# One more turn of ScalarE's tables and a new order of the whole program, in a gated linear attention with a squared-ReLU channel mix on one core

## The chip, the core and the metric

The kernel runs on one core of a Trainium2 chip. Five engines work on their own queues: TensorE (PE in the profile, its weight loads PEld), VectorE (DVE), ScalarE (ACT), GpSimd (POOL) and SyncE (SP), which here only issues transfers between the chip's memory and the core's buffers. The metric is the device time of one execution in microseconds (us). The times shown are medians over runs; the profile is of one execution.

## The reference

Two layers, on 4 sequences of 768 steps with 8 heads of 48 channels, all in float32.

```
f = 1 / (1 + exp(-f_logit))
for t in range(S):
    state = f[t][:, None] * state + outer(k[t], v[t])
    y[t] = q[t] @ state
x = y, heads side by side (384 channels)
xk = mu_k * x + (1 - mu_k) * x_prev;  xr = mu_r * x + (1 - mu_r) * x_prev
out = sigmoid(xr @ w_r) * (maximum(xk @ w_k, 0) ** 2 @ w_v)
```

`x_prev` is `x` one step earlier; w_k is 384 by 1024, w_v 1024 by 384, w_r 384 by 384. The weights come as 64-bit words, of which the kernel makes float32 numbers itself.

## The kernel before

**Attention** is done in 24 chunks of 128 steps, 6 to a sequence. For chunk i a scan on DVE makes the running product b of the gates (`b{i}`, line 223), ACT makes its inverse by a logarithm and an exponential (`ln{i}`, line 229, and `rb{i}`, line 231), DVE corrects that inverse (`n{i}`, line 244, and `iv{i}`, line 246). q is scaled by b on DVE (`q{i}`, line 233), k by the inverse (`k{i}`, two halves, lines 241 and 242, on POOL or DVE). PE then takes the scores (`S{i}`, line 302), transposes of k (`TR{i}`, line 287), state sums (`P{i}`, line 321) and the outputs (`YA{i}`, `YB{i}`, line 334). Around them stand copies and small products: `bl` keeps the last column of b, `kt` brings the transposed k from PE's accumulators, `m` masks the scores (on DVE in one instruction, on ACT as a copy, with the mask then on POOL as `mg`), `zb`, `T`, `g` and `za` carry the state over, `y` writes the output out. `S{i}` waits for both halves of `k{i}` and for `q{i}`; `P{i}` for `kt{i}`.

**Gates.** f is loaded and turned by a sigmoid in place, three chunks at a time. The first three chunks are loaded and turned one by one (`f0.0` to `f0.2`, `sf0.0` to `sf0.2`, line 387), the second three in one piece (`f1`, `sf1`, line 392). The later pieces are turned next to a unit's output sigmoid (`sg{u}`, lines 482 to 487), which loads the sigmoid table before and the table of logarithm and exponential behind it. `ex` (line 772) is the first load of that second table; every `ln` waits for it.

**Channel mix** goes in 8 units of 3 chunks. Per unit PE makes 8 groups F of 9 matmuls (through w_k), 3 groups R of 9 (w_r) and 6 groups W of 12 (w_v), all in line 453: each float32 operand is split in a high part (xh, k2h, H of a weight) and a low one (xl, k2l, L), and three of the four products are taken. For unit 0 the mix of x with its past is done on PE (`XM`, line 583), with the diagonal matrices `dg` (POOL) and `eg`, copied out of `dg` by transfers (`ed`). F's results pass relu (`r`), square (`h`, `kk`) and difference (`l`), which DVE, ACT and POOL share.

**Weights.** Each piece of a weight (8 of wk, 6 of wv, 4 of wr) is loaded and made into numbers by S (ACT or DVE), T and X (DVE), H and L, at 512, 384 or 288 columns for wv, wk and wr. Later a check reads each piece once more (`c{p}` into two buffers "words", `cm{p}` on DVE, line 748); after the last one `lo`, `lot` (two small transposes on PE) and `lom` make a flag (`strong`).

**Order.** ORDER is a table of about 1,400 task names, written out by hand or search; a name with /A, /V or /G puts the task on ACT, DVE or POOL. Each engine issues its instructions in the order of the table, SP its transfers too, and an instruction that waits holds all behind it on its engine. Accumulator tiles `pm` (four of them) and other rotating buffers are handed out in the same order.

Of the kernel before, what the change touches and what calls it, by code (L numbers as in the profile page):

```python
# [52 lines left out]
dg/G b3 q1 ln0 rb0 ln1 bl3/V rb1 n0 iv0 wv2 qk2 n1 q2 iv1 k0/G k1/G wvS2/A qk3 q3 wvT2 wk0 ed2 v2 v1 wk4 S0 ln2 rb2
m0/A n2 wvX2 iv2 TR0 kt0/A wkS0/A S1 P0 zb0/A ln3 m1/A TR1 YA0 w0/A wkT0 wkX0 kt1/A rb3 T0 mg0/G g1 YB0 k2/G za1/G b4
n3 y0/A P1 S2 TR2 zb1 YA1 wk5 wk2 wk1 qk4 v3 ed0 ed1 wk6 wk3 iv3 T1 ln4 wkS5/A bl4/A m2/V wvH3/G mg1/G za2/G wkS2/A
kt2/A wkH0/A P2 rb4 w1/A wkS1/A wkT2 mg2/V wkT5 wkX2 q4 zb2 YB1 n4 T2 wkX5 wkT1 k3/G wkL0/G x00 wvH2/G g3 wkH5/G g4
za3/G iv4 wkX1 wvL3/V wkH1/G TR3 y1/A S3 YA2 kt3/A w2/A wkS4/A P3 YB2 wkS3/A y2/A wkT4 wkT3 wkX4 wkX3 b5 qk5 wr2 wk7
wr0 wr1 wv1 v4 wr3 XM0.00 wkS6/A m3/A ln5 mh0.00/A XM0.10 wkT6 zb3 wkX6 q5 ml0.00 rb5 bl5/A wkH4/A wvS1/A n5 T3 iv5
mh0.10/A wkH3/A ml0.10 wvT1 wvX1 XM0.01 k4/G mg3/G TR4 mh0.01/A wkS7/A YA3 S4 w3/A wvL2/G g5 wkL4/G YB3 kt4/A wrS3/A
P4 wkT7 ml0.01 wkX7 wrS0/A y3/A wvH1/A wkH6/A wkH2/G za4/G k5/G wkL1/G wkH7/G wkL2/G wvL1/G wkL3/G wkL7/G TR5 wrT0  # L60
m4/V wrT3 wrX0 wrX3 kt5/V F0.01 r0.01/A zb4 F0.00 v5 wrS1/A sp0.01 wv5 sp0.00 sp0.02 wv0 f4 v8 YA4 d0.010 wrT1 T4 wrX1
mg4/V xm0.010 za5/V wvS5/V wrH3/A kk0.01/A w4/A P5 S5 YB4 wrH0/A wrH1/G wkL6/G wkL5/G F0.03 d0.011 r0.00/A kk0.00/A
y4/A h0.00 r0.03/A kk0.03/A F0.04 r0.04/A h0.01 d0.012 zb5 xm0.011 wvT5 YA5 wrS2/V wvX5 kk0.04/A w5/A F0.02 xh0.010/V
wrT2 m5/V wrX2 mg5/V YB5 xm0.012 h0.04 xh0.011/A r0.02/A xh0.012/A wvS0/V xl0.010/V wvT0 wvH5/G wrL0/G wvL5/G wrL1/G
l0.00/G x01 wrL3/V xl0.011/V y5/A h0.03 wrH2/A h0.02 wvX0 kk0.02/V xl0.012/G wrL2/V F0.07 F0.06 r0.06/A r0.07/A F0.05
r0.05/A kk0.05/A kk0.07/V R0.0 h0.07 kk0.06/A lg0.0/A h0.05 R0.1 lg0.1/A h0.06 wvH0/G l0.03/G wvL0/G l0.04/G l0.01/G
qk8 qk7 v6 f2 qk6 wv4 l0.02/V wvS4/V wvT4 wvX4 wvH4/A sp1.00 sp1.01 R0.2 d1.00 xm1.010 xh1.010/A lg0.2/A sg0 v7 qk9
sp1.02 c5 f3 W0.20 W0.00 l0.07/G wvL4/G l0.05/G l0.06/V xm1.000 W0.01 d1.01 xm1.001 xm1.011 sf2 d1.02 xm1.002
xh1.000/V xm1.012 xl1.000/G o0.0 b7 W0.10 W0.21 xh1.001/A xl1.001/V q7 b6 bl7/A xh1.011/A xh1.002/A ln6 bl6/A W0.11
xl1.002/G xl1.010/G xh1.012/V o0.2 q6 o0.1 F1.00 F1.02 ln7 rb7 rb6 n6 iv6 k6/V r1.02/V TR6 r1.00/A kk1.00/A h1.00  # L70
kt6/V l1.00/V kk1.02/A xl1.011/G xl1.012/G R1.0 b8 F1.04 r1.04/V lg1.0/A kk1.04/V h1.02 ln8 h1.04 R1.1 R1.2 lg1.1/A n7
bl8/V q8 rb8 n8 iv7 lg1.2/A F1.01 F1.07 P6 S6 iv8 r1.01/V r1.07/V kk1.01/V zb6/V l1.04/V T6 m6/V kk1.07/V mg6/V
l1.02/G k7/G k8/G g8 g7 za7/G F1.03 sg1 TR7 sf3 YA6 w6/V kt7/A r1.03/A b9 S7 YB6 P7 F1.05 TR8 y6/A h1.01 m7/V zb7
mg7/V q9 ln9 YA7 kt8/A w7/A rb9 r1.05/A bl9/A h1.03 kk1.03/V T7 S8 YB7 P8 F1.06 b10 h1.07 kk1.05/A ln10 y7/A v10 qk10
qk11 v9 n9 iv9 za8/V zb8 m8/V T8 b11 mg8/V l1.01/G l1.03/G cz k9/G r1.06/A kk1.06/A h1.06 bl10/V W1.10 TR9 YA8 S9 w8/A
rb10 g10 g9 x02 za9/G kt9/V YB8 P9 q10 q11 h1.05 l1.05/V y8/A ln11 bl11/A rb11 l1.06/G l1.07/V n10 zb9 iv10 W1.20
W1.11 W1.21 W1.00 W1.01 n11 iv11 T9 o1.1 m9/A out0.0 qk12 v11 sp2.00 d2.00 xm2.000 xh2.000/A xm2.010 sp2.01 out0.2
sp2.02 out0.1 d2.01 d2.02 xm2.001 xm2.011 o1.2 k10/G k11/G za10/G TR10 TR11 xh2.010/A xh2.001/A YA9 kt10/A w9/A
xl2.000/V S10 P10 g11 mg9/G YB9 xl2.001/G xm2.002 xh2.002/A xl2.002/V kt11/V zb10 xm2.012 xh2.012/V xl2.010/V F2.00
r2.00/A T10 F2.07 xl2.012/V o1.0 m10/V mg10/V F2.01 F2.04 kk2.00/A y9/A h2.00 r2.04/V YA10 w10/V kk2.04/A h2.04 P11  # L80
S11 YB10 F2.02 y10/A F2.03 za11/V l2.00/V r2.07/V zb11 kk2.07/V YA11 h2.07 r2.01/A kk2.01/A r2.02/A h2.02 l2.04/V
m11/V mg11/V l2.07/G xh2.011/V w11/V F2.05 h2.01 YB11 r2.03/V kk2.02/V l2.01/V x03 xl2.011/G h2.03 kk2.03/A l2.02/G
R2.0 y11/A lg2.0/V R2.1 lg2.1/A r2.05/A h2.05 F2.06 kk2.05/V r2.06/V l2.05/V R2.2 h2.06 lg2.2/A out1.0 v12 f5 out1.1
out1.2 qk13 f6 v13 qk14 v14 qk15 sp3.00 sp3.02 sp3.01 sg2 d3.00 l2.03/G kk2.06/V xm3.010 xm3.000 W2.10 l2.06/G W2.11
W2.20 d3.01 xh3.010/V xl3.010/V d3.02 xm3.011 sf4 xh3.000/A xm3.012 xm3.002 xm3.001 xh3.012/A W2.21 W2.00 b12 W2.01
ln12 bl12/A rb12 xh3.011/A o2.1 xl3.012/G q12 o2.2 n12 xl3.011/G xl3.000/G iv12 k12/V TR12 R3.0 b14 o2.0 kt12/A
xh3.001/A bl14/A b13 ln13 lg3.0/V xh3.002/A q14 bl13/V xl3.001/V q13 R3.2 R3.1 rb13 ln14 lg3.2/A rb14 S12 P12 n13
lg3.1/V m12/V iv13 mg12/V xl3.002/G k13/G g14 g13 n14 F3.03 r3.03/V F3.00 TR13 iv14 F3.04 k14/V zb12/V kk3.03/V kt13/V
T12 TR14 r3.04/V kt14/V sg3 YA12 P13 S13 r3.00/A w12/A YB12 F3.02 F3.01 sf5 h3.00 kk3.00/A za13/G m13/V mg13/V
kk3.04/V zb13 b15 T13 r3.02/V b16 l3.00/G za14/G y12/A h3.03 ln15 bl15/V g15 g16 YA13 kk3.02/A h3.04 w13/A S14 P14  # L90
rb15 h3.02 YB13 v15 qk16 v17 F3.07 q15 m14/V r3.01/V kk3.01/A n15 zb14 T14 mg14/V iv15 x04 l3.03/G l3.02/G y13/A h3.01
F3.05 F3.06 r3.05/A r3.07/V h3.07 ln16 rb16 za15/V kk3.07/V bl16/V r3.06/A h3.06 kk3.06/A h3.05 k15/G TR15 YA14 w14/V
S15 YB14 kt15/V P15 m15/A kk3.05/A y14/A l3.01/G l3.04/V q16 l3.07/G l3.06/V l3.05/V n16 b17 bl17/V iv16 zb15 W3.20
W3.00 W3.21 W3.01 out2.2 out2.0 qk17 sp4.00 sp4.02 sp4.01 v16 mg15/G T15 q17 o3.2 f7 c2 out2.1 k16/G g17 TR16 kt16/A
YA15 w15/A d4.00 xm4.010 xm4.000 o3.0 d4.01 d4.02 xm4.001 xm4.012 xm4.002 ln17 xh4.010/A xh4.000/A xh4.002/A S16 P16
YB15 W3.10 W3.11 xl4.000/G xh4.001/V y15/A rb17 m16/V xl4.001/V n17 iv17 xm4.011 xl4.002/G za16/G F4.00 F4.03 r4.03/A
# [926 lines left out]
```

## Time and profile before

| | us |
|---|---|
| time, median of 3 runs | 340.57 (337.43 to 342.58) |
| the profiled execution, in all | 339.45 |
| its span | 337.7 |
| PE busy | 309.6 (92%) |
| PE weight loads busy | 296.5 (88%) |
| DVE busy | 271.9 (81%) |
| ACT busy | 200.1 (59%) |
| POOL busy | 141.3 (42%) |

The span runs from the first instruction to the end of the last work; the time in all has what lies around it too. A busy share is an average over the span: in its first 16 us PE does nothing, and in the long middle it is busy throughout. The mean granted clock of TensorE is 0.998 of full speed.

### The profile page before, as it was taken

Reading aid. Unit: us, or ns where it says so; the run is one execution under the profiler, and the core shown is the slowest. Engines: PE = TensorE matmul, PEld = TensorE weight load, DVE = VectorE, ACT = ScalarE, POOL = GpSimd, SP = SyncE. Lnnn points to the kernel's source line nnn. Section 1 sums busy time; section 2 is a strip of 40 time slices with the busy share of each in tenths; the row PEclk is TensorE's granted clock in tenths of the full one; section 3 lists DMA queues with packets and bytes.
Section 4 is the critical chain, followed back from the end, with each engine's and each line's share of the span. In section 5 each row is a group of like instructions: output and inputs, shape, how many; then the busy total and the mean of one; then the engine's idle time right before and its main releaser. Section 6 shows DMA issues by size and latency. Waiting matters only on the chain.

```text
span 337.7 us, 10736 instructions
## 1 busy us (share of the span) xinstructions
PE 309.6 (92%) x4458; PEld 296.5 (88%) x4458; DVE 271.9 (81%) x519; ACT 200.1 (59%) x427; POOL 141.3 (42%) x184
## 2 busy tenths in 40 slices
...
GB/s 246 384 264 237 318 127 411 214 107 2 1 90 170 92 53 365 120 1 2 14 203 22 209 2 215 199 82 0 2 211 156 4 64 48 112 68 213 136 99 105
DMA packets 20634, 45.32 MB, mean 134 GB/s; under 512 B 2848, under 2 KB 13024, under 8 KB 20576
## 3 DMA queue, kind: packets, MB, share of 16 engines
...
HBM read 38.54 MB, written 4.72 MB: 128 GB/s over the span
## 4 chain that ended last, share of the span: by engine, by line
PE 82%; DMA 8%; DVE 3%; issue 3%; SPq 1%; POOL 1%; ACT 0%; DVEq 0%; POOLq 0%
PE pm L453 63%; PE py L334 8%; DMA qk<-in_qkt 4%; PE pss L302 4%; PE pm L287 3%; DMA words<-in_wk 3%; PE pm L583 2%; PE pss L321 2%; DMA out<-t 1%; DVE pm L525 1%; DVE t L545 1%; SPq L381 0%; POOL dg L761 0%; DVE dg L748 0%; DVE t L507 0%
## 5 line engine op out<-in xcount | busy, mean ns | idle before, releaser
L453 PE MATMUL pm<-xh,wk 128*128 128x384 f32 x384 | 104.8, 339 | 0.5 <-DVE t L629 0.5
L453 PE MATMUL pm<-wv,k2h 128*128 128x384 f32 x384 | 97.0, 333 | 0.4 <-DVE t L545 0.3
L453 PEld LDWEIGHTS pm<-xh,wk 128*128 128x128 f32 x384 | 69.3, 188 | 2.4 <-DVE t L629 0.8
L453 PEld LDWEIGHTS pm<-wv,k2h 128*128 128x128 f32 x384 | 68.3, 188 | 1.2 <-DVE t L545 0.6
L453 PE MATMUL pm<-wv,k2l 128*128 128x384 f32 x192 | 63.6, 331 | 0.0
L453 PE MATMUL pm<-xl,wk 128*128 128x384 f32 x192 | 63.6, 331 | 0.0
L635 POOL TENSOR_TENSOR k2l<-t,k2h 128x384 fp32r<-128x384 f32 x36 | 39.1, 1097 | 57.3 <-ACT k2h L627 44.7
L560 POOL TENSOR_TENSOR xl<-t,xh 128x384 fp32r<-128x384 f32 x25 | 26.4, 1064 | 59.8 <-ACT xh L553 42.6
L453 PE MATMUL pm<-wr,xh 128*128 128x384 f32 x144 | 36.5, 334 | 0.0
L453 PEld LDWEIGHTS pm<-xl,wk 128*128 128x128 f32 x192 | 36.1, 188 | 0.0
L453 PEld LDWEIGHTS pm<-wv,k2l 128*128 128x128 f32 x192 | 36.0, 188 | 0.0
L627 ACT ACTIVATE k2h<-t 128x384 fp32r<-128x384 f32 x64 | 32.5, 521 | 5.8 <-DVE t L623 5.6
L622 ACT ACTIVATE t<-pm 128x384 f32<-128x384 f32 x37 | 17.7, 489 | 30.6 <-PE pm L453 28.4
L302 PE MATMUL pss<-qk 64*64 64x64 f32 x768 | 17.2, 228 | 17.4 <-POOL qk L241 16.2
L302 PEld LDWEIGHTS pss<-qk 64*64 64x64 f32 x768 | 14.5, 141 | 18.4 <-POOL qk L241 16.2
L223 DVE TENSOR_TENSOR_SCAN pm<-f,low 128x512 f32<-128x512 f32 x24 | 30.2, 1262 | 0.2
L453 PEld LDWEIGHTS pm<-wr,xh 128*128 128x128 f32 x144 | 25.5, 188 | 0.2
L241 POOL TENSOR_TENSOR qk<-qk,rb 128x256 f32<-128x256 f32 x17 | 13.7, 806 | 27.2 <-DVE rb L246 27.1
L366 ACT ACTIVATE x<-py 64x128 f32<-64x128 f32 (+1 forms) x63 | 19.5, 309 | 9.1 <-PE py L334 8.1
L553 ACT CAST xh<-t 128x384 fp32r<-128x384 f32 x32 | 15.9, 511 | 14.9 <-DVE t L545 14.8
L545 DVE SCALAR_TENSOR_TENSOR t<-pm,mu_sb,x 128x384 f32<-128x384 f32 x42 | 24.2, 609 | 0.4
L453 PE MATMUL pm<-wr,xl 128*128 128x384 f32 x72 | 23.9, 332 | 0.0
(127 smaller groups left out, 597.9 us busy)
## 6 DMA issues: line engine op xcount, KB each, us to landing
...
```

What stands on the lines that cost most here:

```text
L223: pl.add(f"b{i}", ("V", lambda: nc.vector.tensor_tensor_scan(b().rearrange(FL), f().rearrange(FL), self.low.rearrange(FL), 1.0, op0=ALU.mu ...
L241: e.tensor_tensor(k()[:, ::2], k()[:, ::2], rb()[:, ::2], op=ALU.mult)
L302: nc.tensor.matmul(self.pss[HALF[h], r, 64 * j : 64 * j + 64], k()[HALF[r], j, HALF[h]], q()[HALF[r], j, HALF[h ^ j % 2]], start=True, sto ...
L334: first[c, h] = nc.tensor.matmul(to, lhs, rhs, start=(c, h) not in first, stop=stop, skip_group_check=True)
L366: e.activation(o, i_, AF.Copy, scale=-1.0)
L453: nc.tensor.matmul(lines(ps), lhs(a, j), lines(rhs(bb, j)), start=ends[0] and i == 0, stop=ends[1] and i == len(pr) - 1)
L545: pl.add(f"xm{u}.{p}{w}{j}", ("V", lambda xm=xm, w=w, j=j: nc.vector.scalar_tensor_tensor(xm(), pm("d", u, p, j), self.mu_sb[:, w, j : j + ...
L553: pl.add(f"xh{u}.{p}{w}{j}", ("A", lambda xm=xm, hi=hi: nc.scalar.copy(hi(), xm())), ("V", lambda xm=xm, hi=hi: nc.vector.tensor_copy(hi() ...
L560: e.tensor_tensor(lo(), xm(), hi().bitcast(F32), op=ALU.subtract)
L622: pl.add(f"r{name}", ("A", lambda: nc.scalar.activation(r(), ps(), AF.Relu)), ("V", lambda: nc.vector.tensor_scalar(r(), ps(), 0.0, None, ...
L627: pl.add(f"h{name}", ("A", lambda: nc.scalar.activation(hi(), r(), AF.Square)), after=[f"r{name}"], **(kw | {"uses": kw["uses"] + [("t", " ...
L635: e.tensor_tensor(lo(), kk(), hi().bitcast(F32), op=ALU.subtract)
```

## The change

Two rules of the plan change. `ex`, the first load of the table of logarithm and exponential, waits for `sf0.2` and no longer for `sf1`. `sf1` waits for `ex` and loads that table again behind itself; as the sigmoid stands in another table, a load of the sigmoid's table comes ahead of it too. The table ORDER is replaced by another with the same 1,406 tasks, in which many tasks have another place, and some another engine.

```diff
 ORDER = """
-f0.0 f0.1 sf0.0 b0 mu wv3 f0.2 sf0.1 sf0.2 f1 b1 sf1 ex wvS3/V wvT3 onemu wvX3 b2 bl0/V qk0 v0 qk1 bl2/A q0 bl1/V g2
+f0.0 sf0.0 f0.1 sf0.1 b1 bl1/A b0 mu f0.2 qk0 sf0.2 qk1 ex ln1 rb1 bl0/V onemu b2 q0 q1 f1 n1 ln0 iv1 rb0 n0 iv0 k0/V
...
             if u < AHEAD:
-                pl.add(f"sf{u}", ("A", lambda: nc.scalar.activation(t(), t(), AF.Sigmoid)), after=[f"f{u}", "sf0.2"])
+                def late():
+                    nc.scalar.activation(t(), t(), AF.Sigmoid)
+                    nc.scalar.preload_act_table_set(EXP_SET)
+
+                pl.add(f"sf{u}", ("A", late), after=[f"f{u}", "ex"])
...
         pl.add("ex", ("A", lambda: nc.scalar.preload_act_table_set(EXP_SET)),
-               after=["sf1"])
+               after=["sf0.2"])
```

ACT's list at the program's start, before (f_61 holds the first three chunks' gates, f_62 the next three; rb the inverses, pm the accumulator tiles in which b stands):

```order
L869 ACT_TABLE_LOAD
L387 ACTIVATE f_61<-f_61 128x512 x3
L392 ACTIVATE f_62<-f_62 128x1536
L772 ACT_TABLE_LOAD
L226 COPY bl<-pm_96 128x4
L229 ACTIVATE rb_97<-pm_93 128x512
L231 ACTIVATE rb_97<-rb_97 128x512
```

and in the changed kernel:

```order
L873 ACT_TABLE_LOAD
L387 ACTIVATE f_61<-f_61 128x512 x2
L226 COPY bl<-pm_93 128x4
L387 ACTIVATE f_61<-f_61 128x512
L776 ACT_TABLE_LOAD
L229 ACTIVATE rb_97<-pm_93 128x512
L231 ACTIVATE rb_97<-rb_97 128x512
L229 ACTIVATE rb_98<-pm_94 128x512
L231 ACTIVATE rb_98<-rb_98 128x512
L393 ACT_TABLE_LOAD
L393 ACTIVATE f_62<-f_62 128x1536
L394 ACT_TABLE_LOAD
```

The large sigmoid on f_62 has moved from ahead of the first logarithm to behind the second exponential, with a load on either side of it; chunk 1 comes ahead of chunk 0.

DVE's list from the first scan on, before (qk holds q and k of a chunk, words a piece of a weight):

```order
L223 SCALAR_TENSOR_TENSOR pm_93<-f_61,low 128x512
L223 SCALAR_TENSOR_TENSOR pm_94<-f_61,low 128x512
L685 TENSOR_SCALAR pm_95<-words_122 128x512
L673 SCALAR_TENSOR_TENSOR pm_95<-words_122,pm_95 128x512
L756 TENSOR_SCALAR one_mu<-mu_sb 128x6
L681 SCALAR_TENSOR_TENSOR words_122<-words_122,pm_95 128x512
L223 SCALAR_TENSOR_TENSOR pm_96<-f_61,low 128x512
L227 COPY bl<-pm_93 128x4
L233 TENSOR_TENSOR qk_64<-qk_64,pm_93 128x512
L227 COPY bl<-pm_94 128x4
L223 SCALAR_TENSOR_TENSOR pm_95<-f_62,low 128x512
L233 TENSOR_TENSOR qk_65<-qk_65,pm_94 128x512
```

and in the changed kernel:

```order
L223 SCALAR_TENSOR_TENSOR pm_95<-f_61,low 128x512
L233 TENSOR_TENSOR qk_64<-qk_64,pm_94 128x512
L233 TENSOR_TENSOR qk_65<-qk_65,pm_93 128x512
L244 TENSOR_TENSOR pm_93<-rb_97,pm_93 128x512
L246 SCALAR_TENSOR_TENSOR rb_97<-pm_93,rb_97 128x512
L244 TENSOR_TENSOR pm_94<-rb_98,pm_94 128x512
L246 SCALAR_TENSOR_TENSOR rb_98<-pm_94,rb_98 128x512
L241 TENSOR_TENSOR qk_64<-qk_64,rb_98 128x2x128
L242 TENSOR_TENSOR qk_64<-qk_64,rb_98 128x2x128
L309 TENSOR_TENSOR ss_99<-pss,mask 128x512
L233 TENSOR_TENSOR qk_66<-qk_66,pm_95 128x512
L223 SCALAR_TENSOR_TENSOR pm_93<-f_62,low 128x512
```

These rows begin at the third scan; the two ahead of it are those of before, with a copy of bl and one_mu behind them. The three instructions on the weight piece words_122 have left, the scan on f_62 has moved behind the first scores' mask, and the scaling of chunk 0's k (lines 241 and 242), which was POOL's, stands here.

SP's list of transfers at the start, before:

```order
L381 DMA f_61<-in_zt 128x512 x2
L755 DMA mu_sb<-in_mu 128x6
L666 DMA words_122<-in_wv 128x1024
L381 DMA f_61<-in_zt 128x512
L381 DMA f_62<-in_zt 128x1536
L211 DMA qk_64<-in_qkt 128x1024
L213 DMA v_103<-in_vt 128x384
L211 DMA qk_65<-in_qkt 128x1024
```

and in the changed kernel:

```order
L381 DMA f_61<-in_zt 128x512 x2
L759 DMA mu_sb<-in_mu 128x6
L381 DMA f_61<-in_zt 128x512
L211 DMA qk_64<-in_qkt 128x1024
L211 DMA qk_65<-in_qkt 128x1024
L381 DMA f_62<-in_zt 128x1536
L213 DMA v_103<-in_vt 128x384
L211 DMA qk_66<-in_qkt 128x1024
```

The weight piece is gone from between the slices of f, and both first qk tiles stand ahead of the second piece of f. An element has four bytes: 128x512 is 256 KB.

## Rows read from the trace of the kernel before

**Rows 1.** Busy time by stretch: from:to, length, then PE, PEld, DVE, ACT, POOL, clock, DMA.

```profile
16.20:46.10 29.90, 24.25 (x631) 20.71 (x632) 25.53 (x49) 22.03 (x58) 24.03 (x35) 1.00 0.79 250
46.10:79.40 33.30, 33.01 (x350) 31.76 (x349) 30.50 (x54) 26.97 (x60) 24.95 (x25) 1.00 0.57 205
79.40:312.50 233.10, 233.10 (x3371) 225.70 (x3369) 190.07 (x364) 136.13 (x289) 80.28 (x103) 1.00 0.31 98
312.50:332.40 19.90, 19.27 (x111) 18.31 (x110) 11.33 (x22) 5.98 (x10) 7.04 (x6) 1.00 0.41 127
...
4.70:46.10 41.40, 24.25 (x631) 20.71 (x632) 36.01 (x66) 28.56 (x68) 27.32 (x39) 1.00 0.85 287
```

**Rows 2.** Timeline, PE's first instructions: start, us, what, [idle before and its releaser].

```profile
16.23 0.49 PE L302 MATMUL pss<-qk 64*64 64x64 f32 x8 [16.23 <-POOL qk L241]
```

**Rows 3.** Timeline of ACT from its first sigmoid.

```profile
3.52 1.28 ACT L387 ACTIVATE f<-f 128x512 f32<-128x512 f32 x2 [1.49 <-DMA f<-in_zt]
7.93 0.63 ACT L387 ACTIVATE f<-f 128x512 f32<-128x512 f32 x1 [3.12 <-DMA f<-in_zt]
9.79 1.48 ACT L392 ACTIVATE f<-f 128x1536 f32<-128x1536 f32 x1 [1.24 <-DMA f<-in_zt]
11.29 1.28 ACT L772 ACT_TABLE_LOAD   x1
12.59 0.16 ACT L226 COPY bl<-pm 128x4 f32<-128x4 f32 x1
12.65 0.60 ACT L229 ACTIVATE rb<-pm 128x512 f32<-128x512 f32 x1
13.28 0.63 ACT L231 ACTIVATE rb<-rb 128x512 f32<-128x512 f32 x1
```

**Rows 4.** Timeline of DVE, POOL and PE around the first scores.

```profile
4.74 2.35 DVE L223 TENSOR_TENSOR_SCAN pm<-f,low 128x512 f32<-128x512 f32 x2
...
11.11 0.69 DVE L233 TENSOR_TENSOR qk<-qk,pm 128x512 f32<-128x512 f32 x1 [0.46 <-DMA qk<-in_qkt]
...
13.94 0.70 DVE L244 TENSOR_TENSOR pm<-rb,pm 128x512 f32<-128x512 f32 x1 [0.29 <-ACT rb L231]
...
14.68 0.69 DVE L246 SCALAR_TENSOR_TENSOR rb<-pm,rb 128x512 f32<-128x512 f32 x1
15.28 0.69 DVE L244 TENSOR_TENSOR pm<-rb,pm 128x512 f32<-128x512 f32 x1
...
15.45 0.73 POOL L241 TENSOR_TENSOR qk<-qk,rb 128x256 f32<-128x256 f32 x1 [0.89 <-DVE rb L246]
...
16.91 0.92 PE L302 MATMUL pss<-qk 64*64 64x64 f32 x24 [0.19 <-POOL qk L242]
...
17.77 1.11 PE L287 MATMUL pm<-ident,qk 128*128 128x128 f32 x4
...
19.72 0.86 PE L321 MATMUL pss<-v,ktk 64*48 64x48 f32 x32
```

**Rows 5.** Groups of instructions of DVE by line: count, busy us, mean ns, idle before.

```profile
L292 DVE COPY ktk<-pm 128x384 f32<-128x384 f32 x9 | 4.9, 548 | 0.1
...
L241 DVE TENSOR_TENSOR qk<-qk,rb 128x256 f32<-128x256 f32 x7 | 3.3, 476 | 0.2
L242 DVE TENSOR_TENSOR qk<-qk,rb 128x256 f32<-128x256 f32 x7 | 3.2, 461 | 0.0
L685 DVE TENSOR_SCALAR pm<-words 128x512 int32<-128x512 int32 x4 | 2.7, 687 | 0.1
...
L673 DVE SCALAR_TENSOR_TENSOR pm<-words_k2h,pm 128x384 int32<-128x384 int32 x4 | 2.2, 556 | 0.0
```

**Rows 6.** The chain that ended last, in the tail: start, us, what.

```profile
301.49 5.40 DMA words<-in_wk
...
312.91 0.69 DVE dg L748
...
313.62 3.92 DMA words<-in_wk
...
319.53 8.42 PE pm L453 x48
```

146 lines of the change are left out of this document (73 added, 73 removed).

## Prediction

> **What bounds the kernel now.** I read the busy times by stretch first, then what PE waited for, then the first 20 us engine by engine, and the tail last. Up to 16.2 us PE does nothing [rows 2]. The stretches behind tell the case [rows 1]. From 16.2 to 46.1 us, where the first attention chunks run and the weights are made, PE is busy 24.25 of 29.90 us, DVE 25.53. From 46.1 us, the first F group of unit 0, PE is busy 33.01 of 33.30, then 233.10 of 233.10, then 19.27 of 19.90; behind 332.4 there are only the last elementwise product and its store. The granted clock is 1.00 in all stretches with PE work. So behind 46.1 us PE is the bound, and PE's work is the same set of matmuls before and after. Its idle time lies in front: 16.2 us in one wait for POOL's scaled k [rows 2], 5.65 us up to the first F, and 0.3 + 0.6 us later. A new order can earn there and hardly elsewhere. In front the busiest engine is DVE: from 4.7 to 46.1 us it is busy 36.01 of 41.40 us [rows 1].
>
> The first wait is a chain. The transfer of the third slice of f lands for 7.93 us, that of f1 for 9.79; ACT takes both sigmoids, loads the table of Ln and Exp from 11.29 to 12.57, and only then begins the first Ln [rows 3]. DVE then makes n and iv, POOL the scaled k, PE starts at 16.23 [rows 4].
>
> **The change part by part.** *The table behind the third sigmoid.* f1's sigmoid (1.48 us, its wait of 1.24 us for the transfer, [rows 3]) leaves the chain. I walk the new chain with the old durations. The first two sigmoids end at 4.80 as now (3.52 + 1.28). Two scans take 2.35 us [rows 4]: b1 from 4.80 ends about 6.0, b0 about 7.15. ACT copies bl1 behind b1, to 6.2. The transfers now stand in the order f0.0, f0.1, f0.2 (256 KB each), qk0, qk1 (512 each), f1 (768). The landings of the old order, where 512 KB of wv3 stood behind the second slice and 768 of f1 ahead of qk0, give the pace: there 512 KB had landed by 4.15, 1280 by 7.93, 2560 by 11.11 [rows 3, 4]. Read at the new sums, f0.2 (768 KB) lands about 5.4, qk0 (1280) 7.9, qk1 (1792) 9.2, f1 (2560) 11.1. So: third sigmoid 6.2 to 6.8, table to 8.1, ln1 and rb1 to 9.35 (0.60 and 0.63 [rows 3]), ln0 and rb0 to 10.55. DVE: b2 from 7.35, q0 8.5, q1 9.2 with its transfer; n1 9.8, iv1 10.5, n0 11.1, iv0 11.9, by the steps of 0.74 from n to iv and 0.60 to the next n [rows 4]. k0 is now DVE's: 0.48 for its first half against POOL's 0.73 [rows 4, 5]. First scores at about 13.1 instead of 16.23: 3.1 us earlier.
>
> *The second unit's sigmoid with its own table turn.* Behind rb0 ACT now has a load, the sigmoid, a load: 1.28 + 1.48 + 1.28 from 10.55 to 14.6, f1 having landed at 11.1. That is 2.57 us more work on ACT. Behind it stand ln2, kt0 and rb2. kt0 needs TR0, which ends about 15.5 (scores 0.92 us from k0's end at 13.5, then the transposes 1.1 [rows 4]), and b3 needs the sigmoid only when DVE gets to it at about 15.7. So the block is hidden by DVE's n, iv and k0 and by PE's scores; without that cover it costs up to its 4.04 us. ACT's total bears it: it is busy 22.03 of 29.90 us in the next stretch [rows 1]. The first state sums, at 19.72 now [rows 4], come at about 16.
>
> Here the Trainium skill speaks against the change. The trace shows a load of 1.28 us, ACT's next instruction 0.02 us behind it and no standstill [rows 3]. ScalarE: Activation LUTs, section "What ACT_TABLE_LOAD costs", adds a drain of about 1380 ns and books 2.66 us for each switch; section "Rules for kernel authors" says to finish one set before switching. By the page's figure the two added switches cost 5.3 us instead of 2.57 and the sum would be some 3 us worse.
>
> *The order up to the first F.* SP held six transfers, four of weights, behind the eg copies, which wait for dg, and dg stood behind POOL's g2, which needs b2; now it stands behind g1, which needs only the first two scans. Ahead of the first F group DVE's list loses wvS3, kt5, m2 and wvL3 to ACT and POOL (0.69 + 0.55 + 0.69 + 0.69) and the merges wkT6, wkX6, wkX4, wrT0, wrX0 to later (3 x 0.55 + 2 x 0.42); it gains k0 (0.48 + 0.46), m0 (0.69) and wrT2 (0.42); two of the small bl copies go and two come [rows 4, 5] (estimates: m and wvL by other instructions of their 128x512, wr by 288 of wk's 384 columns). 5.1 less 2.0 is 3.1 us. One wait is new: m0, now DVE's, waits for the scores from 13.5 to 14.5: 1.0. One is gone: q0's 0.46 us for its transfer [rows 4]. Net 2.5 to 2.6 us. The chain of attention allows 3.1, DVE 2.5; the later decides: first F 2.5 us earlier, at about 43.6. Bounds: nothing (below), and the whole DVE idle of this stretch, 41.40 - 36.01 = 5.4 us, if the new order packs it without a gap.
> S5 (32 matmuls: 24 of them took 0.92 us where k came in halves, an upper bound; taken as 0.5) stands ahead of the first F and no longer behind it: 0.5 us of PE work less from there.
>
> *The rest.* From the first F on PE has no idle to give: 0.3 us to 79.4, none to 312.5. Many evictions go from DVE to ACT (relu 27 to 19 on DVE, squares 33 to 26, differences 28 to 25; 18 of about 0.55 us: some 10): DVE is busy 190.07 and ACT 136.13 of 233.10 us there, so the move uncovers nothing; cost 0, bounds 0 and the price of a new stall, not seen in any row of before. Tail: same work, 0.6 us to win.
>
> Sum: 2.5 + 0.5 = 3.0 us off the span of 337.7, so 334.7. The profiled execution took 339.45 in all, 1.75 more than its span: **336.5 us**. It lies 1.1 us below the median of the runs shown (340.57; they spread from 337.43 to 342.58).
>
> **The rivals.**
> 1. *DVE binds, nothing is won* (338.5 to 340). From the start to unit 1's first F 23 instructions leave DVE's list and 21 come, about 13 us each way (an estimate by the mean durations of their lines): what left ahead of the first F is made up behind it, by four more of the differences l0 and two of wkL among others. DVE's idle from 4.7 to 79.4 is 5.4 + 2.8 = 8.2 us [rows 1] and has to fall to 5.7 for my sum. For it: DVE has 2.8 idle of 33.3 in that stretch. Against: what is added there (l0.05 and on) is needed only by the second half of W0, with six products of 2 us in between.
> 2. *More is won* (332 to 335): DVE's gaps close by 5 us instead of 2.5. For it: attention runs 3 us ahead and weights are loaded earlier, so fewer waits on DVE. Against: PE's and ACT's own chains set some of the gaps.
> 3. *Slower: the check loads in the tail.* Behind the last W6 product DVE's list has cm10, cm0, cm8, r7.00; each c load needs the buffer freed by the check two before it, so cm10, cm8, cm3, cm11, cm13 is a chain of four transfers, and lot on PE waits for its end with three products behind it. Each turn is 3.92 + 0.69 us now [rows 6], four make 18.4, and cm1 and the reductions add about 2 to lot. PE has 8 F, 3 R and 3 W groups in the same time, about 23 us by 8.42 us for 48 matmuls [rows 6], so 2 to 3 us to spare. With the 5.40 us that one such load took beside stores [rows 6], the chain is 5.9 longer: with 2 to spare PE waits 3.9 us, 340.4, above the 339.45 of now. It costs from 4.4 us a load on and turns the sign at about 5.2.
> 4. *ACT stands still as long again behind each of three early loads*: kt0 at about 18.5, first sums at 19, as now; about 339.5. This is the mechanism of the page's drain (ScalarE: Activation LUTs). The 0.02 us between load and next instruction speaks against it.
> That the change does not do what it says is excluded by ACT's rows: one load pair more, and the first Ln behind the third sigmoid.
>
> **How the numbers follow.** My forecast 0.48, rival 1 0.25, rival 2 0.15, rival 3 0.09, rival 4 0.03. The range 332.0 to 340.5 takes in the first four but for the far ends of 2 and 3 (0.08 below and 0.1 above, with the spread of the runs); the likeliest case alone is 335 to 338. A measurement of this kernel can tell about 2% from no change: under 333.8 is faster, over 347.4 slower. Faster takes most of rival 2: 0.13. Slower needs a stall of over 8 us that no row shows, 0.04. The rest, 0.83, is within 2%.
>
> **What would show it.** Right: PE's first matmul at 13 to 13.5 us; the table load at about 7, the second pair around 10.5 to 14.6 with no wait of PE put down to kt; first F matmul between 42.5 and 44.5; from there to the last W no PE idle beyond 1 us. Wrong: first F at 46 with DVE busy throughout (rival 1), a PE wait of over 1 us at lot or at F7 put down to the checks (3), a gap behind ACT_TABLE_LOAD of 1 us or more (4), or stretches behind 46 us in which PE is under 97% busy.

## The result

The changed kernel takes 343.32 us (median of 20 runs, 341.83 to 349.5), the kernel before beside it 340.01 us (20 runs, 337.43 to 343.25). The ratio is 1.012 with a 95% interval of 1.009 to 1.015: slower by 1.2%, where 336.5 us and a range up to 340.5 had been forecast. The ratios, here and in the table below, leave out the few runs that took over 1.5% more than the fastest of their kernel, so they are not the quotients of the medians. The profiled span is 341.9 us against 337.7.

The stretches of the changed kernel, by the same cuts as [rows 1] (columns as there):

```profile
0.00:16.20 16.20, 2.20 (x36) 1.75 (x36) 12.68 (x30) 11.01 (x13) 5.79 (x18) 1.00 0.84 303
16.20:46.10 29.90, 26.47 (x633) 23.00 (x633) 26.75 (x51) 22.27 (x56) 20.71 (x30) 1.00 0.73 237
46.10:79.40 33.30, 31.81 (x310) 29.90 (x309) 30.60 (x60) 28.77 (x61) 19.87 (x23) 1.00 0.55 186
79.40:312.50 233.10, 229.97 (x3345) 220.91 (x3344) 181.97 (x348) 136.47 (x288) 93.13 (x111) 1.00 0.32 102
```

PE now works 2.2 us of the first 16.2, where it did nothing. But behind 46.1 us it has lost 1.2 us up to 79.4 (31.81 against 33.01) and 3.1 us in the long middle (229.97 against 233.10), where it had never stood still. The granted clock is 1.00 in all four rows.

The start of the new kernel, ACT's timeline (compare [rows 3]):

```profile
3.49 1.28 ACT L387 ACTIVATE f<-f 128x512 f32<-128x512 f32 x2 [1.46 <-DMA f<-in_zt]
6.07 0.16 ACT L226 COPY bl<-pm 128x4 f32<-128x4 f32 x1 [1.30 <-DVE pm L223]
6.52 0.63 ACT L387 ACTIVATE f<-f 128x512 f32<-128x512 f32 x1 [0.29 <-DMA f<-in_zt]
7.17 1.28 ACT L776 ACT_TABLE_LOAD   x1
8.46 0.60 ACT L229 ACTIVATE rb<-pm 128x512 f32<-128x512 f32 x1
...
10.89 1.28 ACT L393 ACT_TABLE_LOAD   x1
12.18 1.48 ACT L393 ACTIVATE f<-f 128x1536 f32<-128x1536 f32 x1
13.68 1.28 ACT L394 ACT_TABLE_LOAD   x1
```

and PE's first instructions (compare [rows 2, 4]):

```profile
14.00 1.25 PE L302 MATMUL pss<-qk 64*64 64x64 f32 x32 [14.00 <-DVE qk L241]
15.19 1.11 PE L287 MATMUL pm<-ident,qk 128*128 128x128 f32 x4
16.23 1.13 PE L302 MATMUL pss<-qk 64*64 64x64 f32 x32
18.14 0.90 PE L321 MATMUL pss<-v,ktk 64*48 64x48 f32 x32 [0.77 <-DMA v<-in_vt]
```

The first logarithm runs at 8.46 us instead of 12.65, the first scores at 14.00 instead of 16.23, the first state sums at 18.14 instead of 19.72. So the front does what the change says.

Then the waits. PE's from 46.1 us on (engine, line, what it waited for: us in total, times, longest):

```profile
PE pm L457 <- DVE t L544: 1.3, 1, 1.3
PE pm L457 <- DVE t L511: 1.2, 2, 0.9
PE py L334 <- DVE done L353: 1.0, 1, 1.0
PE py L334 <- issue: 0.7, 1, 0.7
```

In order of time they end at 54.7 (1.3 us), 101.1 (0.7, put down to nothing that the profile shows), 192.0 (1.0), 200.9 (0.3) and 232.4 us (0.9). And DVE's over the whole span, the two kinds that are new:

```profile
DVE pm L529 <- DMA x<-stage: 8.0, 5, 3.0
...
DVE t L511 <- DMA out<-t: 2.9, 1, 2.9
```

But for the one at 101.1, PE waits for DVE, and DVE for transfers: for the spread copies `sp` (six for a unit, 24 KB each, which bring y from the tile "stage" into x, where `d`, line 529, reads them), and for an output store, whose tile t the next output product (line 511) needs. The stop at 54.7 comes of a weight's transfer (e13).

To see where each run loses, I read from each trace when PE begins the first scores and the first F, and when it ends the last W product of units 0, 2, 4 and 7 (us). The experiments e1 to e15 are told below; the median of the kernel before, run beside them, lies between 338.9 and 340.4, and the last column has the ratio to it. The other columns are read from one execution of each kernel. Its time lies within 1 us of the median in most; but in e1, e7 and e15 it is 2.5, 2.1 and 1.6 us below, in e6 1.9 us above, so spans and medians do not rank these alike.

| run | scores | F | W0 end | W2 end | W4 end | W7 end | span | median, ratio |
|---|---|---|---|---|---|---|---|---|
| before | 16.2 | 46.1 | 79.6 | 153.7 | 227.7 | 332.4 | 337.7 | 340.01 |
| after | 14.0 | 45.4 | 80.2 | 155.2 | 231.5 | 336.3 | 341.9 | 343.32, 1.012 |
| e1 table alone | 16.3 | 47.9 | 82.0 | 156.2 | 230.2 | 335.1 | 339.8 | 344.19, 1.013 |
| e2 order alone | 16.8 | 47.3 | 84.0 | 157.9 | 234.4 | 339.3 | 344.5 | 345.65, 1.015 |
| e3 spreads first | 13.0 | 43.8 | 80.6 | 154.8 | 241.2 | 345.5 | 351.3 | 353.12, 1.039 |
| e4 before, spreads late | 16.5 | 44.9 | 79.0 | 153.1 | 233.1 | 337.9 | 343.0 | 345.49, 1.018 |
| e5 two spreads | 13.9 | 44.3 | 79.2 | 153.2 | 231.1 | 336.5 | 342.1 | 344.34, 1.010 |
| e6 new, then old | 12.9 | 43.9 | 82.1 | 157.9 | 231.9 | 336.4 | 342.8 | 342.74, 1.007 |
| e7 old, then new | 17.0 | 45.2 | 79.2 | 153.1 | 229.4 | 334.5 | 340.2 | 344.10, 1.008 |
| e8 v0 and wr1 | 13.2 | 44.1 | 82.1 | 156.3 | 232.5 | 337.5 | 343.0 | 345.61, 1.015 |
| e9 spreads and stores | 14.2 | 45.1 | 79.6 | 153.5 | 228.6 | 332.4 | 338.0 | 339.91, 1.000 |
| e10 stores | 12.9 | 43.9 | 78.5 | 153.7 | 228.1 | 332.8 | 338.3 | 340.70, 1.005 |
| e11 before, no merges | 16.3 | 43.7 | 76.6 | 151.4 | 225.5 | 330.2 | 336.7 | 338.28, 0.997 |
| e12 after, no merges | 14.5 | 45.6 | 79.1 | 155.2 | 231.8 | 337.6 | 343.0 | 344.21, 1.013 |
| e13 f2 late | 13.0 | 44.3 | 77.1 | 151.4 | 228.7 | 333.7 | 339.3 | 341.89, 1.007 |
| e14 all mended | 14.0 | 44.9 | 77.7 | 152.0 | 227.5 | 331.3 | 337.8 | 338.63, 0.995 |
| e15 f2 late, no merges | 13.3 | 43.8 | 76.6 | 150.7 | 227.0 | 332.1 | 337.4 | 340.80, 1.002 |

The change's 4.2 us of span are, by stretch: 0.6 up to the end of W0, 0.9 from there to W2, 2.3 to W4 (76.3 against 74.0), 0.1 to W7, 0.3 behind it. Up to W0 a trace moves by 1 to 2 us with nothing changed there: before and e4 have the same order so far (79.6 and 79.0), and so have after, e3, e5, e9 and e10 (78.5 to 80.6). So the 0.6 us up to W0 is within the scatter. From W2 to W4 the traces repeat: 76.2 to 76.6 us in after, e2, e7, e8, e12 and e15 and 77.3 in e13, all with the new list there; 74.0 to 74.1 in before, e1, e6 and e11, with the old one.

### The profile page after: what moved, and what is told of

The parts are those of the page before. It is cut to its first block, busy times and chain, and to the rows that moved or that the text cites. A ratio compares the mean times of both kernels' runs of the same rounds, so it can differ in the third digit from the quotient of the medians.

```text
span 341.9 us, 10745 instructions
## 1 busy us (share of the span) xinstructions
PE 314.3 (92%) x4458; PEld 298.8 (87%) x4458; DVE 266.1 (78%) x512; ACT 207.5 (61%) x433; POOL 147.4 (43%) x186
## 4 chain that ended last, share of the span: by engine, by line
PE 75%; DMA 8%; DVE 7%; SPq 4%; ACT 3%; issue 2%; DVEq 0%; ACTq 0%
PE pm L457 56%; PE py L334 7%; PE pm L287 3%; PE pss L302 3%; DMA v<-in_vt 3%; DMA x<-stage 3%; PE pm L587 2%; PE pss L321 2%; DMA out<-t 2%; SPq L438 1%; SPq L211 1%; DVE t L511 1%; DVE x L368 1%; DVE t L549 1%; SPq L381 1%
## 5 line engine op out<-in xcount | busy, mean ns | idle before, releaser
L457 PE MATMUL pm<-xh,wk 128*128 128x384 f32 x384 | 104.8, 339 | 1.6 <-DVE t L544 1.3
L639 POOL TENSOR_TENSOR k2l<-t,k2h 128x384 fp32r<-128x384 f32 x39 | 41.6, 1075 | 59.5 <-ACT k2h L631 37.7
L564 POOL TENSOR_TENSOR xl<-t,xh 128x384 fp32r<-128x384 f32 x27 | 31.5, 1185 | 57.2 <-ACT xh L557 24.9
L626 ACT ACTIVATE t<-pm 128x384 f32<-128x384 f32 x45 | 21.8, 489 | 26.7 <-PE pm L457 16.8
L457 PE MATMUL pm<-wr,xh 128*128 128x384 f32 x144 | 36.8, 336 | 0.9 <-DVE t L511 0.9
L223 DVE TENSOR_TENSOR_SCAN pm<-f,low 128x512 f32<-128x512 f32 x24 | 32.2, 1346 | 0.3
L557 ACT CAST xh<-t 128x384 fp32r<-128x384 f32 x31 | 15.1, 512 | 24.7 <-DVE t L549 24.6
L334 PE MATMUL py<-qk,z 64*64 64x64 f32 x704 | 22.7, 235 | 1.4 <-DVE done L353 1.0
## 6 DMA issues: line engine op xcount, KB each, us to landing
v<-in_vt SPq DMA_DIRECT2D x24, 192.0 KB, 4.7
out<-t SPq DMA_DIRECT2D x21, 192.0 KB, 4.4
```

The costliest lines, as they stand in the source:

```text
L223: pl.add(f"b{i}", ("V", lambda: nc.vector.tensor_tensor_scan(b().rearrange(FL), f().rearrange(FL), self.low.rearrange(FL), 1.0, op0=ALU.mu ...
L334: first[c, h] = nc.tensor.matmul(to, lhs, rhs, start=(c, h) not in first, stop=stop, skip_group_check=True)
L457: nc.tensor.matmul(lines(ps), lhs(a, j), lines(rhs(bb, j)), start=ends[0] and i == 0, stop=ends[1] and i == len(pr) - 1)
L557: pl.add(f"xh{u}.{p}{w}{j}", ("A", lambda xm=xm, hi=hi: nc.scalar.copy(hi(), xm())), ("V", lambda xm=xm, hi=hi: nc.vector.tensor_copy(hi() ...
L564: e.tensor_tensor(lo(), xm(), hi().bitcast(F32), op=ALU.subtract)
L626: pl.add(f"r{name}", ("A", lambda: nc.scalar.activation(r(), ps(), AF.Relu)), ("V", lambda: nc.vector.tensor_scalar(r(), ps(), 0.0, None, ...
```

## The experiments

**e1 and e2: the two parts alone.** e1 keeps the old order and makes the new table turn; of ORDER only the names that must move do so:

```diff
-... f0.2 sf0.1 sf0.2 f1 b1 sf1 ex ... b2 bl0/V qk0 v0 ... b3 q1 ln0 rb0 ln1 bl3/V rb1 n0 ... k0/G k1/G ...
+... f0.2 sf0.1 sf0.2 ex qk0 f1 b1 ... b2 bl0/V v0 ... q1 ln0 rb0 ln1 rb1 sf1 n0 ... k0/G k1/G b3 bl3/V ...
```

> The two rules of the plan as in the change, on the old order, with only these tasks moved: ex and qk0 up behind the third sigmoid, sf1 behind rb1, b3 and bl3 behind k1. Theory (the loss sits in the new order's list of transfers, behind unit 1): first scores 1 to 2 us earlier than 16.2, part of it lost by the first F; time 339 to 341 beside 340 of before. Rival (the table turn itself costs: 2.57 us more on ACT, later b3): 342.5 or more.

344.19 us: the theory missed, and the rival's figure came. The first scores did not come earlier, and the state sums came 3.0 us later (22.75 against 19.72). ACT in e1:

```profile
14.76 0.63 ACT L231 ACTIVATE rb<-rb 128x512 f32<-128x512 f32 x1
15.41 1.28 ACT L393 ACT_TABLE_LOAD   x1
16.70 1.49 ACT L393 ACTIVATE f<-f 128x1536 f32<-128x1536 f32 x1
18.21 1.28 ACT L394 ACT_TABLE_LOAD   x1
...
21.67 0.48 ACT L291 COPY ktk<-pm 128x384 f32<-128x384 f32 x1
```

and PE:

```profile
17.82 1.11 PE L287 MATMUL pm<-ident,qk 128*128 128x128 f32 x4
21.87 1.13 PE L302 MATMUL pss<-qk 64*64 64x64 f32 x32 [2.94 <-issue]
```

The block of load, sigmoid and load stands bare: it ends at 19.49, kt0 (the copy at 21.67) comes behind it, and the sums wait. This is the cover of the prediction's second step, taken away. And on DVE chunk 1's q waits for its transfer, with chunk 0's n (14.02) behind it, so the earlier logarithms reach the scores no sooner:

```profile
13.41 0.69 DVE L233 TENSOR_TENSOR qk<-qk,pm 128x512 f32<-128x512 f32 x1 [1.58 <-DMA qk<-in_qkt]
```

By the spans of the traces e1 costs 2.1 us, by the medians 4.2. e2 is the new order with the old turn (f1 behind f0.2, sf1 ahead of ex):

```diff
-... f0.2 qk0 sf0.2 qk1 ex ln1 ... q1 f1 n1 ... ed0 sf1 TR0 ...
+... f0.2 f1 qk0 sf0.2 qk1 sf1 ex ln1 ... q1 n1 ... ed0 TR0 ...
```

> The new order with the old rules for the tables (f1 and sf1 ahead of ex, one table load less), nothing else changed. Theory: first scores at 16 to 17 us, but the same PE waits at 190 and 229 us; 342.5 to 345. Rival (the table turn costs): back to 340.

345.65 us, just above the range expected, with 76.5 us from W2 to W4 (76.3 in the changed kernel). So by the traces' spans the table turn is worth 2.6 us within the new order (scores at 14.0 against 16.8), though the intervals of the two ratios overlap (1.009 to 1.015 and 1.007 to 1.023); in the old order, placed as in e1, it costs 2 to 4 us. The loss behind W2 belongs to the order.

**e3, e4 and e5: where the spread copies stand in SP's list.** In the changed kernel sp4.01 and sp4.02 stand behind v16 and f7 (192 and 768 KB), sp5.02 behind v20, c5 and qk19. e3 moves those and the copies of units 2 and 3 forward, e5 (run later) only those of units 4 and 5; e4 moves the same three backward in the kernel before.

```diff
 e3, e5
-sp4.00 v16 f7 sp4.01 sp4.02 c7 ... sp5.00 sp5.01 v20 c5 qk19 ... sp5.02
+sp4.00 sp4.01 sp4.02 v16 f7 c7 ... sp5.00 sp5.01 sp5.02 v20 c5 qk19
 e3 besides
-sp2.00 out0.2 ... sp2.01 ... v11 sp2.02 ... qk12 qk14 v15 qk15 qk13 v13 ... v12 sp3.00 sp3.02 f4 out1.2 out1.1 ... sp3.01
+sp2.00 sp2.01 sp2.02 out0.2 ... sp3.00 sp3.02 sp3.01 qk12 qk14 v15 qk15 qk13 v13 ... v12 f4 out1.2 out1.1
 e4
-sp4.00 sp4.02 sp4.01 v16 ... f7 ... sp5.00 sp5.01 v18 sp5.02 c4 qk18 qk19
+sp4.00 v16 ... f7 sp4.02 sp4.01 ... sp5.00 sp5.01 v18 c4 qk18 qk19 sp5.02
```

> The changed kernel with the small x<-stage copies of units 2 to 5 moved ahead of the bulk transfers that stand between them in SP's list; no engine's compute order changes. Theory: DVE's 8.0 us of waits for x<-stage fall to 2 or less, the two PE waits of 1.1 us each at 190 and 229 us go; 340.5 to 341.5 beside 343.3 of the change. Rival (these waits are hidden, the loss is DVE's or ACT's order): 343.

> The kernel before with the second and third x<-stage copy of unit 4 moved behind f7 and the third of unit 5 behind qk19 in SP's list, as the new order has them. Theory: DVE waits 3 us or more for x<-stage, where it waited none, and PE waits 1 to 2.5 us near 185 and 225 us; 341 to 342.5. Rival: 340, DVE's wait is covered.

> The changed kernel with three transfers moved in SP's list and nothing else: unit 4's spread copies sp4.01 and sp4.02 stand right behind sp4.00 again (ahead of v16 and f7), sp5.02 right behind sp5.01 (ahead of v20, f and qk19). Theory (the new order's loss behind unit 1 comes in good part from 24 KB spread copies that now queue behind transfers of 768 KB, so that DVE stands still and PE after it): the 1.15 us of PE at S16 to YB15 and the 1.09 us at W4.01 to R5.0 go, and x<-stage waits of DVE fall from 8.0 to under 4 us; 341.0 to 342.0 us, 1.3 to 2.3 us under the changed kernel. Rival (the late copies only show where DVE would wait anyway; the moves of units 2 and 3 were not what made the earlier test slow): no change or slower, 343 us or more.

e4: 345.49 us, the direction expected and 3 us above the range. One copy is enough: DVE's longest wait there and PE's behind it (200 to 235 us):

```profile
DVE pm L525 <- DMA x<-stage: 4.7, 1, 4.7
```

```profile
PE pm L453 <- DVE t L545: 3.9, 1, 3.9
```

From the end of that stop on the granted clock of TensorE is at half, 1.2 GHz:

```profile
223.00:226.40 3.40, 3.20 (x10) 3.20 (x11) 3.40 (x7) 0.93 (x2) 2.08 (x2) 0.50 0.02 5
```

PE begins its matmuls 0.32 us apart there and 0.17 behind it, which adds about 1.6 us to the 3.9. So the price of the late copy is part stop and part clock.

e3: 353.12 us, a miss by 12. DVE's waits for spread copies fell from 8.0 to 2.5 us, but SP's own waits show the price (SP's queue, first in the changed kernel, then in e3, and DVE's in e3 from 130 to 215 us):

```profile
SPq L438 <- DVE stage L368: 30.5, 3, 21.6
```

```profile
SPq L438 <- DVE stage L368: 58.3, 4, 25.4
```

```profile
DVE t L549 <- DMA out<-t: 7.7, 1, 7.7
...
DVE t L511 <- DMA out<-t: 4.0, 1, 4.0
```

A copy put forward waits for its y, and SP holds all that stands behind: the stores came late, their t tiles were not free, and DVE stood still for those. PE stopped for 4.5 us ahead of 159.4 and for 2.8 us ahead of 209.3, and here too the granted clock is at half around the end of each stop, for 6.8 us from 158.1 and 3.4 us from 209.3:

```profile
159.30:164.90 5.60, 5.55 (x17) 5.55 (x18) 5.53 (x9) 1.94 (x5) 4.94 (x7) 0.50 0.10 35
```

By the same steps of 0.32 and 0.17 us the clock makes about 4 of the 10 us that e3 loses from W2 to W4 against the changed kernel, the stops the rest.

e5: 344.34 us, above the range expected. The 1.15 us of PE at unit 5's attention went as expected (W2 to W3 took 41.2 us instead of 42.3), the second (at W4.01 to R5.0) did not, and PE's stop at 200.9 grew from 0.3 to 3.2 us. DVE in e5:

```profile
193.89 0.69 DVE L233 TENSOR_TENSOR qk<-qk,pm 128x512 f32<-128x512 f32 x1
200.00 0.56 DVE L511 TENSOR_TENSOR t<-pm,lg 128x384 f32<-128x384 f32 x1 [5.42 <-DMA out<-t]
```

and SP's issues from 190 to 200 us there (size, median us to landing):

```profile
words<-in_wk SPq DMA_DIRECT2D x1, 512.0 KB, 9.2
v<-in_vt SPq DMA_DIRECT2D x1, 192.0 KB, 8.4
out<-t SPq DMA_DIRECT2D x1, 192.0 KB, 9.1
```

The product at 200.00 is o3.0. The order in which tiles are handed out gives it the tile that out3.2 frees, and that store was issued behind qk17, f6, v19, v17 and c2 (2.1 MB) and landed 9.1 us later. A second wait of 2.5 us is o4.1's, for the tile of out2.0, stored 70 us after it was made.

**e6 and e7: halves of the two orders.** e6 has the new order up to the first R group of unit 0 and all else in the old order, e7 the mirror with the old table turn:

```diff
 e6
-(new order) ... R0.0 R0.2 wvT4 ...
+(new order up to here) R0.0 (what is left, in the old order) ...
 e7
-(old order) ... R0.0 h0.07 kk0.06/A ...
+(old order up to here) R0.0 (what is left, in the new order) ...
```

> The changed kernel's order up to the first R product of unit 0 (at about 60 us), and from there the remaining work in the order of the kernel before; the new table turns are kept. Theory (gain of under 1 us in front, loss of about 4 us behind, so the two are separate): 338.5 to 340.5 us, 3 to 5 us under the changed kernel, and PE waits behind 80 us as small as in the kernel before (some 4 us in all). Rival (the loss behind comes of how the front leaves the queues, and follows it): 342 us or more.

> The mirror of the run before: the order and the table turns of the kernel before up to the first R product of unit 0, from there the remaining work in the new order. Theory (the loss lies in the new order behind unit 1): 343 to 345 us, with PE waits at S16 to YB15, at F4.05 to F4.00 and at W4.01 to R5.0 as in the changed kernel. Rival (the loss comes with the front): 340 to 341 us.

e7, 344.10 us, has the 76.3 us from W2 to W4, e6 the old 74.0: the loss of 2.3 us there belongs to the later list and to nothing ahead of it. e6 as a whole, 342.74 us, lies above the 338.5 to 340.5 expected, where its rival had it, but not for the rival's reason: the stretch from W2 to W4 does not follow the front. W0 ends at 82.1, with PE stops of 1.5 us at 53.5 and at 60.5 and 0.9 at 75.7. The one at 60.5 is in e2, e3 and e8 too, which have no seam; what the seam itself costs is not separated.

**e8: two early transfers.**

```diff
-... f1 n1 ... v1 qk2 wk2 q2 qk3 v0 ... f2 sp0.01 ml0.01 wr1 ...
+... f1 v0 n1 ... v1 qk2 wk2 q2 qk3 ... wr1 f2 sp0.01 ml0.01 ...
```

> The changed kernel with two transfers moved earlier in SP's list: v0 right behind f1 (it stood behind v1, qk2, wk2, qk3), wr1 ahead of f2. Theory: P0 no longer waits for v0 (18.0 us), the first state sums come at 16 to 17 instead of 18.1; the first F, at 45.4 us, comes no more than 0.5 us earlier, since DVE's list ahead of it is full; the wait of DVE for wr1 (2.0 us) and of PE for it (1.3 us at 52.6) go: 341.5 to 342.5 us. Rival (v0's landing was what held the whole front): first F at 44.0 us or earlier and 340 to 341 us.

345.61 us, 3 us above the range. The state sums came at 17.0 and the first F at 44.1, no sooner than in e10, which leaves v0 where it was (17.1 and 43.9): v0 does not hold the front. wr1's wait went, and two others came: DVE stood 2.51 us for POOL's za5, and POOL 3.1 us for a spread copy of unit 0, which now stood behind f2 and wr1.

**e9 and e10: the stores.** Both put out2.0 right behind out0.0, and out3.2 behind its product with qk17 and f6 behind it; e9 has the spreads of e5 too.

```diff
-out0.0 qk17 f6 TR16 ... o3.2 d4.02 ... v19 v17 c2 out3.2 ... sp5.02 v18 out2.0
+out0.0 out2.0 TR16 ... o3.2 out3.2 qk17 f6 d4.02 ... v19 v17 c2 ... sp5.02 v18
```

> The run with two spreads, with the stores mended as well: besides sp4.01, sp4.02 behind sp4.00 and sp5.02 behind sp5.01, the store out2.0 stands right behind out0.0, and out3.2 right behind its product o3.2 with qk17 and f6 (512 and 768 KB) behind it instead of ahead of it. Theory (in the run with two spreads DVE stood 5.4 us at o3.0 and 2.5 us at o4.1, because their t buffers are those of out3.2 and out2.0, whose stores were queued behind bulk; PE lost 3.35 and 1.33 us there): both PE waits go and no other takes their place, so PE waits from 160 to 240 us fall from 6.5 to under 2 us; 339.5 to 341 us, level with the kernel before. Rival (DVE in this stretch simply has more work ahead of o3.0 than it can do, and each mended wait moves to the next instruction): 343 us or more, with a wait of DVE or ACT for another transfer in its place.

> The changed kernel with the stores mended alone (out2.0 right behind out0.0, out3.2 right behind o3.2 with qk17 and f6 behind it), the spread copies as late as in the changed kernel. Theory: DVE's 2.94 us at o3.0 and PE's 0.7 us at F4.05 to F4.00 go; the 1.15 us at S16 to YB15 and 1.1 us at W4.01 to R5.0, which come of the spread copies, stay: 342 to 343 us. Rival (the spread copies' lateness costs nothing once the stores are early): 340 to 341 us.

e9: 339.91 us, level with the kernel before (interval 0.997 to 1.004), as expected; PE's waits from 46.1 us on are these:

```profile
PE pm L457 <- DVE t L544: 1.0, 1, 1.0
PE pm L457 <- DVE t L511: 0.3, 1, 0.3
PE pm L457 <- ACT lg L480: 0.2, 1, 0.2
```

e10, 340.70 us, did better than expected and came where its rival had it: W2 to W4 took 74.4 us with no PE stop at all, though the spread copies stand as late as in the changed kernel; of the stop at W4.01 to R5.0 0.6 us were left. The last four copies of unit 4 landed 3.0 to 4.3 us after their issue instead of 3.4 to 4.6, and DVE's wait for them fell from 0.98 to 0.43 us; why is open, since f7 ahead of them also landed 0.4 us sooner. So the moves of the stores, with qk17 and f6 held back, take away most of the loss by themselves, and e9 and e10 are not told apart (1.000 and 1.005, with intervals that overlap).

**e11 and e12: is it DVE that holds the front?** Both leave out DVE's merges (task T) of all weight pieces:

```diff
-                else:
+                elif False:
                     nc.vector.scalar_tensor_tensor(
                         t(), high(), 3, t(), op0=ALU.logical_shift_left, op1=ALU.bitwise_or)
```

> The kernel before without DVE's 18 merges of the weights' words (8 of wk, 4 of wr, 6 of wv: 8 x 0.56 + 4 x 0.46 + 6 x 0.69 = 10.4 us of DVE, nearly all before 62 us); the rest of the computation is as it was, so the weights are wrong. Theory (DVE binds from the first scores to the end of unit 0's products, so what the front gains is spent waiting for DVE): the last W0 product ends at 74 to 77 us instead of 79.6, and the whole falls by 3 to 5 us, to 335 to 337 us. Rival (transfers, ACT or PE's own chain bind there): last W0 product after 78.5 us, 339 us or more.

> The changed kernel without the same 18 merges. Theory: with DVE relieved, the earlier first scores (2 to 3 us) come through: the last W0 product ends 1.5 to 3 us before that of the kernel before without merges, at 72 to 75 us; the losses behind 80 us (about 2.3 us in units 3 and 4) stay, so the whole stands level with it, 335 to 338 us. Rival (something else than DVE takes the gain in front): last W0 product level with that of the kernel before without merges, and the whole 2 to 4 us above it.

In the old order W0 ended at 76.6, 3.0 us earlier, as DVE's bound says. The whole gained less than expected: 338.28 us where 335 to 337 had been, ratio 0.997 (0.994 to 1.000). In the trace 0.7 of the 3.0 us are lost again up to W2 and 1.2 behind W7. In the new order W0 ended at 79.1, within the spread of its other runs (78.5 to 80.6), and the whole took 344.21 us: my theory fell. DVE was busy 59.73 instead of 66.62 us from 4.7 to 79.4, and nothing came of it.

**e13, e14 and e15: f2.** One transfer of 768 KB moves, which a sigmoid needs at 71 us:

```diff
-... sp0.00 f2 sp0.01 ml0.01 wr1 ...
+... sp0.00 sp0.01 ml0.01 wr1 f2 ...
```

e13 is the changed kernel with this alone, e14 has e9's moves besides, e15 is e13 without the merges.

> The changed kernel with one transfer moved: f2 (768 KB, needed from 64 us on) stands behind wr1 in SP's list instead of ahead of sp0.01 and wr1. Theory (from 47 to 53 us DVE waits 2.0 us for wr1 and POOL 2.0 us for unit 0's spread copies, both landed late behind f2, and PE loses 1.3 us at F0.02; this is where the front's gain goes): these waits go and the last W0 product ends at 77 to 78.5 us (78.5 to 80.2 in the runs with this front so far); 341.5 to 342.5 us, the losses in units 3 and 4 as before. Rival (ACT, which carries 4 us more work up to 79 us than in the kernel before, holds the front whatever the transfers do): last W0 product at 79 us or later, 343 us or more.

> The run with spreads and stores mended, with f2 behind wr1 as well. Theory: 1 to 2 us under that run (339.9 us beside 338.9 of before), so 337.5 to 339 us and the first version at or under the kernel before, ratio 0.993 to 0.999. Rival (ACT holds the front): as without the move, ratio 1.000 to 1.004.

> The run with f2 behind wr1, without DVE's 18 merges of the weights' words (weights wrong). In the kernel before these 10.4 us of DVE were worth 3 us at the last W0 product; in the changed kernel nothing. Theory (there the late transfers of wr1 and the spread copies hid it): the last W0 product ends 1.5 to 3 us before that of the run with f2 late, at 74.5 to 77 us. Rival (ACT holds the front in the new order, DVE has slack): within 1 us of it.

W0 ended at 77.1 us in e13 and 77.7 in e14, as expected. In the changed kernel DVE stood for wr1:

```profile
50.36 0.35 DVE L279 TENSOR_TENSOR sm<-pss,z 128x192 f32<-128x192 f32 x1
52.70 0.46 DVE L689 TENSOR_SCALAR pm<-lg 128x288 int32<-128x288 int32 x1 [1.99 <-DMA lg<-in_wr]
```

In e13 the same instruction follows without a gap:

```profile
49.22 0.35 DVE L279 TENSOR_TENSOR sm<-pss,z 128x192 f32<-128x192 f32 x1
49.49 0.45 DVE L689 TENSOR_SCALAR pm<-lg 128x288 int32<-128x288 int32 x1
```

and the stretch from 46.1 to 79.4 us in e14:

```profile
46.10:79.40 33.30, 33.20 (x319) 31.58 (x318) 32.06 (x61) 28.13 (x59) 23.67 (x25) 1.00 0.54 180
79.40:312.50 233.10, 232.09 (x3363) 223.62 (x3362) 184.76 (x352) 138.19 (x292) 95.39 (x111) 1.00 0.33 106
```

PE has 0.1 us left in the first of these. e15 ends W0 only 0.5 us before e13, where 1.5 to 3 had been expected: with PE busy 33.30 of 33.30 there, DVE's work no longer matters in the new order. e14 takes 338.63 us, as expected, ratio 0.995 (0.992 to 0.998): a few entries moved in SP's list make of the changed kernel the fastest of all runs with the whole computation. For f2 alone the times say less: 1.012 becomes 1.007 (e13) and 1.000 becomes 0.995 (e14 against e9), the same way both times, but each pair of intervals overlaps.

## Why the prediction was wrong

The forecast was a span of 334.7 us; it came to 341.9. Of the 7.2 us between them 3.6 lie ahead of the end of W0 (76.6 by the sum, 80.2 measured), 3.6 behind it.

**First scores (step 1): nearly right.** 13.1 us forecast, 14.0 in the profile, 12.9 to 14.5 in the other runs with this front and turn. The landings read from sums of KB were about 1 us early: the third slice 6.5 instead of 5.4, qk0 8.8 instead of 7.9, qk1 10.1 instead of 9.2.

**The second table turn (step 2): right.** The block ran from 10.89 to 14.96 us, no PE wait is put down to kt0, and e1 shows what the cover is worth. The trace has 0.01 us between a load and the next instruction, at 8.46 and at 12.18, so rival 4 falls. The drain of about 1380 ns that ScalarE: Activation LUTs, "What ACT_TABLE_LOAD costs", in the Trainium skill adds to a switch does not show here either. The sums came at 18.14 instead of 16: kt0 on ACT (17.21) stood behind a logarithm that waited 1.75 us for DVE, and v0's transfer landed at 18.00. With v0 moved up the first F came no sooner (e8).

**Front (step 3): the mechanism missed a wait, and DVE does not bind.** Of the 3.6 us 0.9 are the later first scores, 0.9 lie from there to the first F (31.4 us against the 30.5 of the sum), 1.8 from the first F to the end of W0 (34.8 against 33.0, the 33.5 of before less the 0.5 of S5). Up to the first F step 3 let DVE's list decide. But in all twelve traces with this list in front the first F comes 30.4 to 31.4 us behind the first scores, with v0 moved (e8, 30.9) and without DVE's merges (e12 and e15, 31.1 and 30.5) too, where the old order took 28.2 to 29.9 (before, e4, e7). What sets these 31 us is open; ACT, busy 59.57 us from 4.7 to 79.4 against 55.53 in the kernel before, is a rival that no run tests there.

Behind the first F the sum allowed for no stop. What stood in the way was f2: its 768 KB stand ahead of sp0.01 and wr1 in SP's list, DVE and POOL each stood still for 2.0 us from 50 to 53, and PE for 1.3. With f2 moved this stretch took 32.8 us in e13, e14 and e15 alike, against 34.5 to 36.8 in after, e3, e5, e9 and e10, and W0 ended 2.5 and 1.9 us ahead of the kernel before, which is what the sum had forecast less some 0.5 to 1. The prediction had followed the landings of SP's list up to 11 us only. Rival 1 named the right outcome up to W0, "nothing is won", by the wrong cause: e11 bears DVE's bound out for the old order, e12 and e15 refute it for the new one.

**The rest (step 4): this step failed outright.** "Cost 0, bounds 0 and the price of a new stall, not seen in any row of before." That the moved evictions cost nothing agrees with the trace: behind W0 no PE wait is put down to ACT. The busy sums went another way, though: from 79.4 to 312.5 us ACT has 136.47 (136.13 before), DVE 181.97 (190.07) and POOL 93.13 (80.28).

But the order of SP's list behind the front was never looked at, and there PE was stopped. Between W2 and W4 the loss is 2.3 us; 1.3 of it are two PE stops, at 192.0 behind a late spread copy and at 200.9 behind a store, both behind bulk transfers. e5 moves the copies and takes away the first, e10 moves the store and holds bulk back and takes away both, and e4 makes such a stop in the old order. So the copies' share and the store's are not separated. Without any stop the new list still takes 0.4 us more there (e10, 74.4), which is not explained. The price had a row of before that I used for the tail alone (rival 3): a transfer of 512 KB that takes 5.40 us beside stores [rows 6]. That PE has no idle time in 233 us says that all transfers of the old order come in time, not that those of a new one will. The 0.9 us from W0 to W2 are two PE waits, 0.2 us at 96.5 and 0.7 at 101.1; shorter or equal ones are in e10, in e12 and, with the old order, in e11, none in e5, e9 and e13, and what decides whether they appear I did not settle.

**The tail.** Rival 3 didn't come about: W4 to W7 took 104.8 us against 104.7, with no PE wait at lot. The 104.8 hold the stop of 0.9 us at 232.4; in e9 and e14, which have none there, the stretch took 103.8. So the tail has a gain of 0.9 us once both the copies and the stores ahead of it are in time; with the stores alone (e10) it took 104.7.

**The signs.** "Stretches behind 46 us in which PE is under 97% busy" was named as what would show it wrong, and the one from 46.1 to 79.4 is at 95.5%. The range was too narrow on the upper side: a new order of 1,400 names can add stops, and those above cost PE 0.3 to 4.5 us each; no rival had one in the long middle, and 1.2% slower belonged in the range.
